# Batch 0 through the general attention path, four heads of batch 1's keys pooled on GpSimd in the head, and first value products in single PSUM banks

## The chip, the core and the metric

The kernel runs on one core of a Trainium2 chip. The core has a matrix engine (TensorE, PE in the profile, with its weight loads as PEld), a vector engine (DVE), a scalar engine (ACT), GpSimd (POOL) and a queue engine (SP). PE writes only to PSUM, which the kernel uses as four tiles of one bank (p1a to p1d) and two tiles of two banks each (p2, named p in the profile). Loads that change fp32 to bf16 on the way are issued by GpSimd; SP issues loads and stores without a change of type. The metric is the device time of one execution in microseconds, the median over several runs; lower is better.

## The reference

Eight batches, eight heads, 576 rows, head size 64. Keys and values are averaged over groups of 8 rows, so that 72 remain; attention is taken against these, and a mixer over tokens and channels follows. Cut to what matters:

```python
k_p = k.reshape(B, H, 72, 8, D).mean(axis=3)
v_p = v.reshape(B, H, 72, 8, D).mean(axis=3)
attn = softmax(q @ k_p.transpose(0, 1, 3, 2) / sqrt(D))
x = (attn @ v_p).transpose(0, 2, 1, 3).reshape(B, S, H * D)
h = relu(x.transpose(0, 2, 1) @ w_tok1) @ w_tok2        # tokens: 576 -> 256 -> 576
u = x + h.transpose(0, 2, 1)
out = u + relu(u @ w_ch1) @ w_ch2                       # channels: 512 -> 1536 -> 512
```

## The kernel before

All engines run an order written out by hand: the program emits steps one after the other, and each engine carries out its own instructions in just that order, waiting by semaphores for the others. The order comes from two tables. `HEAD` (line 21) lists what comes first: loads (words with L), dummy matmuls that keep PE busy (d with a count), and the whole attention and token mixing of batch 0. `PLAN` (line 22) has one row per unit. Unit n is the channel mixing of batch n (a ninth unit takes the last 64 rows of all batches together). It issues 12 tiles of the first layer, `l1_tile` (line 514, matmuls on line 517), and then 84 groups of quarter products of the second layer (line 583), which use sums and differences of halves so that fewer products are needed. Each of its `yield`s has a number, and the row of `PLAN` says which steps of the next batches are emitted at that number: "1.s0" is step s0 of batch 1. Unit n carries the attention of batch n + 1 and the pooling of batch n + 2.

Steps of a batch, by their names in both tables:

- `lk`, `lq`, `lv`: GpSimd issues the loads of keys, queries and values (lines 118 and 128). At a key or value load a second, small transfer brings rows 64 to 72.
- `K0`, `K1`, `V0`, `V1`: pooling of four heads by three adds on GpSimd (`pool8`, lines 171 to 180); `v1` is the same on DVE. `kpool` (line 250) pools all keys by 8 matmuls with the identity on PE, `vpool` (line 259) four heads of values.
- `Q0`, `Q1`: one block transpose on DVE for four heads of queries (line 284). `kpT`: four PE transposes of the pooled keys, copied by ACT (line 219).
- `s0`, `s1`, `s2`: scores and exponentials (line 289). Each takes both p2 tiles; its matmuls use four groups of 32 rows of the PE array (line 297). s0 and s1 do columns 0 to 384 of heads 0 to 3 and 4 to 7, s2 the last 192 columns of all heads.
- `av`: products with the values, with the division by the row sums on DVE (lines 370 to 387). In the head these go by four heads: `a00` is group 0, row chunks 0 and 1 (`avh`, line 325), `m01` the matching part of the token layer (`ath`, line 348). `X` and `A` (lines 464 to 480) make the transposed input of unit 0, with PE adding x and the token layer in PSUM.
- `w0` to `w3`: differences of halves of w_ch2 on DVE (line 563); "=1" to "=4": sums of halves of the hidden layer (line 552). `g`: a gate, by which GpSimd waits for a point in DVE's order (line 715).

Batch 0 has its own path to the scores. SP loads two pairs of heads of the queries as fp32 (line 742), ACT and DVE turn them to bf16 (c0 and c1, line 694), and GpSimd loads the other two pairs (line 700). PE pools the keys (`kp2`, line 227) and transposes them against a zero-padded tile (`kt2`, line 238), so that even and odd rows of a pair have their own stationary tile. PE transposes the queries too (`qT`, line 271), and `score` (line 309) does one pair of heads and one parity with two matmuls and one exponential.

Queues: GpSimd issues nearly all loads, in the order of the L words and of the `l` steps, mixed with its pooling and gates. SP has only the two fp32 loads in the head, and later the stores. The L words of the head are, in order: keys in three pieces (kA, kT, kB), late queries, values in three pieces, w_tok1 (four transfers), batch 1's keys, w_tok2, and then parts of w_ch1 and w_ch2 among batch 1's queries and values.

Of the kernel before, what the change touches and what calls it, by code (L numbers as in the profile page):

```python
# [8 lines left out]
FP32 = mybir.dt.float32  # L9
BF16 = mybir.dt.bfloat16  # L10
U32 = mybir.dt.uint32
AF = mybir.ActivationFunctionType
ALU = mybir.AluOpType
# [7 lines left out]
HEAD = """LkA LkT LkB Lq LvA LvT LvB Lt1 Lk1 Lt2 Lc1a Lq1 Lc1b Lc1c Lv1 Lc2b Lc1d p1 Lc2a Lc2c d4 c0 prep d3 c1 d4 d2 d1 q0 d2 kp0 kp1 kt0 q1 kt1 o0 kp2 o1 q3 e1 kt2 e0 q2 e3 vpool0 o3 d1 d1 a00 e2 vpool1 o2 a02 m01 d1 a04 m00 a12 m03 X1 m02 a10 m04 X0 p0 a14 1.kpool m11 m12 m14 m13 m10 A1 X3 A0 X2 A2 A3"""  # L21
PLAN = [
# [13 lines left out]
def kernel(  # L36
# [60 lines left out]
    qf = area2[:, 0:4 * BR * D].bitcast(FP32).rearrange("p (a n) -> p a n", a=2)  # L97
    f2 = area2[:, 2304:2304 + 2 * S].rearrange("p (c n) -> p c n", c=2)
    warm = area2[:, 3584:4096]
# [3 lines left out]
    kpz = area[0:SP, 0:1536].rearrange("j (h e d) -> j h e d", h=H, e=3)  # L103
    kT = area[:, 2048:2048 + 2 * H * SP].rearrange("m (o k) -> m o k", o=2)
    qT0 = area[:, 3200:3200 + 2 * HP * EV].rearrange("m (a l n) -> m a l n", a=HP, l=2)

# [23 lines left out]
    def first_kv(key, part):  # L130
        if (0, key) not in loaded:
            loaded[0, key] = raw.tile([SP, H, POOL, D], BF16, name=key + "r")
        h0, h1, j0, j1 = {"A": (0, HP, 0, BP), "B": (HP, H, 0, BP), "T": (0, H, BP, SP)}[part]
        kv(loaded[0, key], k if key == "k" else v, 0, h0, h1, j0, j1)

    def q_pairs(a0, a1):
        return q[0, 2 * a0:2 * a1].rearrange("(a l) (p r) d -> (l p) a (r d)", l=2, r=BR)
# [49 lines left out]
    def batch_steps(b):  # L187
# [5 lines left out]
        def prepare():  # L193
            kp = att.tile([SP, 2, 2, 4, D // 2], BF16, name="kp") if b >= 1 else None
            st.update(kp=kp, vp=values[par], ex=exps[par], xt=rests[b // 2 % 2])
            if not first:
                st["kD"] = att.tile([P, 2, 2, SP], BF16, name="kD")
# [20 lines left out]

        def kpT():
            ps = take([P, 4, SP], BF16)  # L220
            for i in range(4):
                nc.tensor.transpose(out=ps[:, i, :], in_=st["kp"][:, i // 2, i % 2].rearrange("j l d -> j (l d)"),
                                    identity=ident[0:SP, 0:SP])
            nc.scalar.copy(out=st["kD"].rearrange("p g e j -> p (g e j)"), in_=ps.rearrange("p i j -> p (i j)"))
            give(ps)

        def kp2(h0, h1):
            def go():
                ps = take([P, 512], FP32)
                n = (h1 - h0) * D  # L230
                for i in range(POOL):
                    nc.tensor.matmul(out=ps[0:SP, 0:n], lhsT=ident[0:SP, 0:SP], rhs=loaded[b, "k"][:, h0:h1, i, :],
                                     start=(i == 0), stop=(i == POOL - 1))
                nc.vector.tensor_copy(out=kpz[:, h0:h1, 1, :], in_=ps[0:SP, 0:n].rearrange("j (h d) -> j h d", d=D))
                give(ps)
            return go

        def kt2(h0, h1):
            def go():
                ps = take([P, 2, h1 - h0, SP], BF16)  # L240
                for odd in range(2):
                    for h in range(h0, h1):
                        nc.tensor.transpose(out=ps[:, odd, h - h0, :],
                                            in_=kpz[:, h, 1 - odd:3 - odd].rearrange("j e d -> j (e d)"),
                                            identity=ident[0:SP, 0:SP])
                nc.vector.tensor_copy(out=kT[:, :, h0 * SP:h1 * SP], in_=ps.rearrange("m o h j -> m o (h j)"))
                give(ps)
            return go
# [10 lines left out]
        def ppool(g):  # L259
            def go():  # L260
# [7 lines left out]
                give(ps)  # L268
            return go

        def qT(hp):
            def go():
                ps = take([P, NE, 2, BP], BF16)
                for rr in range(NE):
                    nc.tensor.transpose(out=ps[:, rr].rearrange("m l p -> m (l p)"),
                                        in_=loaded[b, "q"][:, hp, rr * P:(rr + 1) * P], identity=ident)
                nc.vector.tensor_copy(out=qT0[:, hp].rearrange("m l (r p) -> m r l p", p=BP), in_=ps)
                give(ps)
            return go
# [29 lines left out]
        def score(hp, odd):  # L309
            n = OD if odd else EV  # L310

            def go():
                ps = ps_two.tile([P, 2, 512], FP32, name="p2")
                exv = st["ex"][:, 0:H * S].rearrange("j (h n) -> j h n", h=H)[:, 2 * hp:2 * hp + 2]
                for hl in range(2):
                    h = 2 * hp + hl
                    keys = slice(h * SP, (h + 1) * SP)
                    nc.tensor.matmul(out=ps[0:SP, hl, 0:n], lhsT=kT[:, odd, keys], rhs=qT0[:, hp, hl, 0:n],
                                     start=True, stop=True)
                dst = exv.rearrange("j h (r p) -> j h r p", p=BP)[:, :, odd:BR:2, :]  # L320
# [466 lines left out]
```

## Time and profile before

| what | value |
|---|---|
| median of 3 runs | 265.07 us (264.4 to 265.51) |
| the profiled execution | 264.03 us |
| its span, first to last instruction | 262.2 us |
| granted TensorE clock | 1.00 |
| DMA, mean over the span | 131 GB/s, 34.29 MB |
| DMA from 20 to 50 us | 205 to 207 GB/s |
| chain that ended last | PE 80%, GpSimd 8%, DMA 7%, DVE 3% |

How to read the views: a line of the chain of waits has the start, the length and the work that the end of the kernel hung on at that time. A line of the timeline has the start, the busy time, engine, source line, operation, output and input tiles, their shapes and a count; in brackets stands how long the engine had been idle and what ended that. Busy time is not time on the path: matmuls overlap, so that one of 512 columns is shown as 379 ns while the next starts 216 ns after it. Rows of 40 digits cut the span into slices of 6.55 us, and each digit is the busy share in tenths. The time of a load "to landing" is counted from its issue.

### The profile page before, as it was taken

To read this page: it belongs to the slowest core of one execution; us is meant where nothing else is said; L and a number is where in the kernel's file an instruction comes from. 1 tells how busy PE (TensorE), PEld (TensorE's weight loads), DVE (VectorE), ACT (ScalarE), POOL (GpSimd) and SP (SyncE) were. 2 spreads that over 40 slices of the span, in tenths; PEclk is the share of its full clock that TensorE was granted. 3 is DMA by queue.
4 is the path that set the end of the run, shared out by engine and by line. 5 is a ranking of instruction groups with operands and counts; after the bars stand their busy time and mean duration, and the time that the engine had idled before them with its cause. 6 is when DMAs were issued, how large, how long until landed. Compare 5 with 4: busy or idle time off the path is not lost.

```text
span 262.2 us, 5324 instructions
## 1 busy us (share of the span) xinstructions
PE 255.8 (98%) x2121; PEld 160.4 (61%) x2121; DVE 179.7 (69%) x370; ACT 119.2 (45%) x195; POOL 150.0 (57%) x177
## 2 busy tenths in 40 slices
PE   8899999999999999999999999999999999999994
PEld 3775556754658545864487448744774486486483
DVE  4566489998786657993899449964795486175183
ACT  2445754149465554435641584155535502612610
POOL 8576145999989999999939881988000000101000
PEclk9999999999999999999999999999999999999999
DMA  7999999992096839699357840831414054503204
GB/s 150 191 200 205 206 206 208 207 223 77 2 172 101 133 118 201 146 196 261 66 154 125 239 133 2 162 92 41 123 35 127 5 158 113 129 0 88 75 0 160
DMA packets 31704, 34.29 MB, mean 131 GB/s; under 512 B 3136, under 2 KB 23744, under 8 KB 31680
## 3 DMA queue, kind: packets, MB, share of 16 engines
q0 software_dynamic: 17632, 17.64, 42.6%
q1 hardware_dynamic: 13632, 15.93, 20.4%
q10 hardware_dynamic: 416, 0.39, 0.5%
q8 instruction: 16, 0.26, 0.4%
q14 instruction: 8, 0.07, 0.1%
HBM read 38.99 MB, written 12.58 MB: 197 GB/s over the span
## 4 chain that ended last, share of the span: by engine, by line
PE 80%; POOL 8%; DMA 7%; DVE 3%; issue 1%; POOLq 0%
PE p1d L517 9%; PE p1c L517 9%; PE p1a L517 8%; PE p1b L517 7%; PE p1b L583 7%; PE p1c L583 7%; PE p1a L583 6%; DMA qb<-in_q_dram 5%; PE p1d L583 4%; PE p L297 3%; PE p L379 3%; POOL t L174 2%; POOL t L175 2%; DMA kr<-in_k_dram 2%; PE p L583 2%; PE p1d L393 2%
## 5 line engine op out<-in xcount | busy, mean ns | idle before, releaser
L717 POOL COPY flag<-flag 1x1 f32<-1x1 f32 x47 | 12.6, 269 | 94.5 <-DVE flag L716 94.5
L517 PEld LDWEIGHTS <-w_ch 128*128 128x128 bf16 x432 | 39.6, 98 | 43.4 <-issue 1.8
L583 PEld LDWEIGHTS <-area 128*128 128x128 bf16 x432 | 40.9, 98 | 7.4 <-issue 1.2
L306 ACT ACTIVATE ex<-p 72x768 bf16<-72x768 f32 x42 | 31.6, 803 | 15.9 <-PE p L297 15.7
L583 PEld LDWEIGHTS <-GT 128*128 128x128 bf16 x324 | 30.8, 98 | 8.2 <-issue 2.4
L175 POOL TENSOR_TENSOR t<-t 72x512 f32<-72x512 f32 x23 | 31.0, 1346 | 1.8
L521 ACT ACTIVATE GT<-p1d 128x512 bf16<-128x512 f32 x29 | 17.3, 597 | 27.0 <-PE p1d L517 21.4
L517 PE MATMUL p1d<-uT,w_ch 128*128 128x512 bf16 x104 | 28.8, 379 | 0.0
L174 POOL TENSOR_TENSOR t<-kr 72x1024 f32<-72x1024 bf16 x12 | 25.9, 2155 | 0.5
L517 PE MATMUL p1c<-uT,w_ch 128*128 128x512 bf16 x96 | 26.1, 379 | 0.0
L521 ACT ACTIVATE GT<-p1b 128x512 bf16<-128x512 f32 x26 | 15.6, 598 | 23.2 <-PE p1b L517 16.8
L517 PE MATMUL p1a<-uT,w_ch 128*128 128x512 bf16 x92 | 25.3, 379 | 0.0
L517 PE MATMUL p1b<-uT,w_ch 128*128 128x512 bf16 x92 | 24.2, 379 | 0.0
L174 POOL TENSOR_TENSOR t<-vr 72x1024 f32<-72x1024 bf16 x11 | 24.1, 2187 | 0.3
L521 ACT ACTIVATE GT<-p1a 128x512 bf16<-128x512 f32 x26 | 15.5, 596 | 11.8 <-PE p1a L517 9.2
L521 ACT ACTIVATE GT<-p1c 128x512 bf16<-128x512 f32 x27 | 16.1, 598 | 8.7 <-PE p1c L517 8.3
L384 DVE TENSOR_TENSOR x<-p,den 128x512 bf16<-128x512 f32 x28 | 19.4, 692 | 1.0
L557 DVE TENSOR_TENSOR area<-GT 128x1536 bf16<-128x1536 bf16 x9 | 9.8, 1086 | 12.4 <-ACT GT L521 12.4
L545 DVE TENSOR_TENSOR area<-GT 128x1536 bf16<-128x1536 bf16 x9 | 10.6, 1178 | 10.1 <-ACT GT L521 7.7
L379 PEld LDWEIGHTS <-ex 72*128 72x128 bf16 x280 | 13.4, 98 | 5.6 <-DVE flag L716 0.4
L583 PE MATMUL p1c<-area,area 128*128 128x256 bf16 x120 | 15.4, 273 | 0.0
L379 PE MATMUL p<-vp,ex 72*128 72x65 bf16 x280 | 14.6, 194 | 0.0
(188 smaller groups left out, 461.1 us busy)
## 6 DMA issues: line engine op xcount, KB each, us to landing
out_dram<-o SPq DMA_DIRECT2D x32, 256.0 KB, 4.0
qb<-in_q_dram POOLq DMA_DIRECT2D x7, 576.0 KB, 9.3
kr<-in_k_dram POOLq DMA_DIRECT2D x7, 512.0 KB, 7.4
vr<-in_v_dram POOLq DMA_DIRECT2D x7, 512.0 KB, 9.8
w_ch<-in_moe_w_ch_dram POOLq DMA_DIRECT2D x5, 512.0 KB, 15.8
mem<-u SPq DMA_DIRECT2D x10, 256.0 KB, 2.0
v<-mem SPq DMA_DIRECT2D x20, 128.0 KB, 2.8
area<-in_q_dram SPq DMA_DIRECT2D x2, 288.0 KB, 3.0
```

The costliest lines, as they stand in the source:

```text
L174: eng.tensor_tensor(out=t4[:, 0:n], in0=t[:, hs, 0:4], in1=t[:, hs, 4:8], op=ALU.add)
L175: eng.tensor_tensor(out=t4[:, 0:n, 0:2], in0=t4[:, 0:n, 0:2], in1=t4[:, 0:n, 2:4], op=ALU.add)
L297: nc.tensor.matmul(out=pss[l // 2][0:SP, l % 2, o:o + n1 - n0], lhsT=st["kD"][quad, g, db, :], rhs=st["qD"][quad, g, n0:n1, db], start=(db ...
L306: nc.scalar.activation(out=dst, in_=src, func=AF.Exp, scale=scale)
L379: nc.tensor.matmul(out=ps[:, h // 4, (h % 4) * (D + 1):(h % 4 + 1) * (D + 1)], lhsT=st["ex"][:, h * S + n0:h * S + n0 + P], rhs=st["vp"][: ...
L384: nc.vector.tensor_tensor(out=dst.rearrange("p (a h d) -> p a h d", a=2, d=D), in0=view[:, :, :, 0:D], in1=den[rows, :, :, None].broadcast ...
L517: nc.tensor.matmul(out=ps, lhsT=w_ch1[:, kk, m * P:(m + 1) * P], rhs=uT[kk], start=(kk == 0), stop=(kk == 3))
L521: nc.scalar.activation(out=GT[:, m, :], in_=ps, func=AF.Relu)
L545: nc.vector.tensor_tensor(out=out, in0=a, in1=b, op=ALU.subtract)
L557: nc.vector.tensor_tensor(out=S4[:, 0], in0=GT[:, f, hi], in1=GT[:, sec, hi], op=ALU.add)
L583: nc.tensor.matmul(out=ps[i] if split else ps[:, i], lhsT=chunk(u, i, a(m)), rhs=w(m), start=start and m == 0 and (i == 0 or split), stop= ...
L717: nc.gpsimd.tensor_copy(out=flag[:, 1:2], in_=flag[:, 0:1])
```

## The change

Batch 0 loses its own path and goes by `Q`, `kpT` (in two halves, h0 and h1) and `s0` to `s2` like the others. SP now loads the fp32 keys of heads 0 to 3 (tile `kf`, in two transfers: rows 0 to 64 and 64 to 72), and DVE pools them from there by three adds (k0). GpSimd loads all queries of batch 0 in two pieces (Lqa, Lqb) and the keys of heads 4 to 7, which PE pools (kp2). Batch 1's keys are pooled half by PE in the head (1.kp2 in place of 1.kpool) and half by GpSimd in the head (1.K0, after p1 and before the issues of the last four weight loads). The first value product (f00 in place of a00) writes each row chunk to its own one-bank tile, with its own reciprocal and product on DVE. The head's order and all rows of `PLAN` are new; the steps in `PLAN` are the same as before, with three gates fewer. Loads in the head: w_tok2 now comes before batch 1's keys, c1b before batch 1's queries, and c1d before c2b. The diff, cut to its core:

```diff
-HEAD = """LkA LkT LkB Lq LvA LvT LvB Lt1 Lk1 Lt2 Lc1a Lq1 Lc1b Lc1c Lv1 Lc2b Lc1d p1 Lc2a Lc2c d4 c0 prep d3 c1 d4 d2 d1 q0 d2 kp0 kp1 kt0 q1 kt1 o0 kp2 o1 q3 e1 kt2 e0 q2 e3 vpool0 o3 d1 d1 a00 e2 vpool1 o2 a02 m01 d1 a04 m00 a12 m03 X1 m02 a10 m04 X0 p0 a14 1.kpool m11 m12 m14 m13 m10 A1 X3 A0 X2 A2 A3"""
+HEAD = """Lqa LkB LkT Lqb LvT LvA prep LvB Lt1 Lt2 Lk1 Lc1a Lc1b Lq1 Lc1c Lv1 p1 1.K0 Lc1d Lc2b Lc2a Lc2c d4 k0 d4 d2 d2 d3 h0 Q0 s0 kp2 Q1 h1 d2 s2 vpool0 d2 a02 f00 vpool1 s1 m03 a04 m01 X0 m02 a10 p0 m04 m00 X1 a12 a14 m11 m10 A0 1.kp2 m12 m13 m14 X2 A1 A2 X3 A3"""
 PLAN = [
-    {0: "0.u3 1.Q0 2.lk 1.kpT", 3: "0.u1", 4: "1.s0 g g", 5: "1.Q1", 9: "1.s1 0.u0", 10: "1.vpool1 1.vpool0 g", 11: "1.s2", 12: "=3 0.u2 2.lq", 13: "1.av1", 14: "1.av3", 16: "1.av2", 18: "w0 3.lk", 19: "1.av0 3.lq", 20: "1.av4 w1 g", 23: "1.at1 2.lv", 24: "1.at0 3.lv =1", 25: "=2 =4", 26: "g", 28: "w3", 31: "1.u1 1.u2", 32: "1.t1", 33: "1.t2 w2", 34: "2.K0", 35: "1.u0", 38: "3.Q1 2.K1", 40: "1.u3", 41: "1.t0", 42: "g", 43: "2.Q0 1.t3", 44: "1.u4 2.V0 2.kpT"},
+    {0: "0.u0 2.lk g 0.u3", 1: "1.kpT", 2: "1.Q0", 3: "g", 4: "2.lq", 6: "2.lv 1.s0", 9: "1.Q1 0.u2", 10: "1.s1", 11: "0.u1 1.vpool1 1.s2", 12: "1.vpool0 =3", 13: "1.av1", 15: "1.av3 3.lv", 16: "1.av2 w0", 20: "g 3.lq 1.av0", 21: "1.av4", 22: "w1 g", 23: "=1 1.at0", 24: "=2 3.lk 1.at1", 25: "w3", 26: "g =4", 28: "2.K0 2.K1", 31: "1.u3", 33: "1.u0", 34: "1.u1", 35: "2.V0", 36: "w2", 37: "1.t3", 40: "1.u2", 42: "1.t0 2.Q0", 43: "1.t2 1.t1", 44: "1.u4"},
...
+    kf = area2[0:SP, 0:2 * HP * POOL * D].bitcast(FP32).rearrange("j (h i d) -> j h i d", i=POOL, d=D)
...
+    def q_group(b, g):
+        return q[b, 4 * g:4 * g + 4].rearrange("l (j n) d -> (l j) (n d)", n=2 * BR)
...
+        def kpT_half(g):
+            def go():
+                ps = take([P, 2, SP], BF16)
+                for e in range(2):
+                    nc.tensor.transpose(out=ps[:, e, :], in_=st["kp"][:, g, e].rearrange("j l d -> j (l d)"),
+                                        identity=ident[0:SP, 0:SP])
+                nc.scalar.copy(out=st["kD"][:, g], in_=ps)
+                give(ps)
+            return go
...
+        def kp_sbuf():
+            pool8(nc.vector, kf, slice(0, HP), st["kp"][:, 0], True)
+
+        def kp_psum():
+            ps = take([P, 512], FP32)
+            for i in range(POOL):
+                nc.tensor.matmul(out=ps[0:SP, 0:HP * D], lhsT=ident[0:SP, 0:SP], rhs=loaded[b, "k"][:, HP:H, i, :],
+                                 start=(i == 0), stop=(i == POOL - 1))
+            nc.vector.tensor_copy(out=st["kp"][:, 1].rearrange("j e l d -> j e (l d)"),
+                                  in_=ps[0:SP, 0:HP * D].rearrange("j (n e) -> j e n", e=2))
+            give(ps)
...
+        def avh_one(g, c):
+            def go():
+                for cc in (c, c + 1) if c < 4 else (4,):
+                    ps = take([P, 4, D + 1], FP32)
+                    den = outp.tile([P, 2, 4], FP32, name="den", bufs=4)
+                    for h in range(4):
+                        n0 = (4 * g + h) * S + cc * P
+                        nc.tensor.matmul(out=ps[:, h, :], lhsT=st["ex"][:, n0:n0 + P], rhs=st["vp"][:, 4 * g + h, :],
+                                         start=True, stop=True)
...
+                    nc.vector.reciprocal(out=den[rows, 0], in_=ps[rows, :, D])
+                    nc.vector.tensor_tensor(out=dst[:, g * 256:(g + 1) * 256].rearrange("p (h d) -> p h d", d=D),
+                                            in0=ps[rows, :, 0:D],
+                                            in1=den[rows, 0, :, None].broadcast_to([rows.stop, 4, D]), op=ALU.mult)
+                    give(ps)
+            return go
...
+        name["k0"], name["kp2"] = kp_sbuf, kp_psum
...
+    def first_q(g):
+        nc.gpsimd.dma_start(out=quarters(loaded[0, "q"])[:, g], in_=q_group(0, g))
...
-        for a in range(2):
-            nc.sync.dma_start(out=qf[:, a:a + 1, :], in_=q_pairs(a, a + 1))
+        for j0, j1 in ((0, BP), (BP, SP)):
+            nc.sync.dma_start(out=kf[j0:j1].rearrange("j h i d -> j h (i d)"),
+                              in_=k[0, 0:HP].rearrange("h (j i) d -> j h (i d)", i=POOL)[j0:j1])
```

Removed with it: `kp2`, `kt2`, `qT`, `score` and the tiles `kpz`, `kT` and `qT0` of batch 0's own path, the two casts c0 and c1, and two of DVE's memsets. The rows of units 1 to 8 of `PLAN`, cut here, hold the same steps in another order. Of these, the prediction speaks of 2.kpT, which moves from step 44 of unit 0 to step 0 of unit 1.

More of the change, by code (lines that the diff above doesn't have):

```diff
@@ L96 @@
     area2 = early.tile([P, 6 * 1024], BF16, name="area2")
-    qf = area2[:, 0:4 * BR * D].bitcast(FP32).rearrange("p (a n) -> p a n", a=2)
-    f2 = area2[:, 2304:2304 + 2 * S].rearrange("p (c n) -> p c n", c=2)
-    warm = area2[:, 3584:4096]
+    kf = area2[0:SP, 0:2 * HP * POOL * D].bitcast(FP32).rearrange("j (h i d) -> j h i d", i=POOL, d=D)
+    f2 = area2[:, 4608:4608 + 2 * S].rearrange("p (c n) -> p c n", c=2)
+    warm = area2[:, 4096:4608]
     uT_tails = singles.tile([P, 4, 4 * P], BF16)
@@ L102 @@
     area = early.tile([P, 6 * 1024], BF16, name="area")
-    kpz = area[0:SP, 0:1536].rearrange("j (h e d) -> j h e d", h=H, e=3)
-    kT = area[:, 2048:2048 + 2 * H * SP].rearrange("m (o k) -> m o k", o=2)
-    qT0 = area[:, 3200:3200 + 2 * HP * EV].rearrange("m (a l n) -> m a l n", a=HP, l=2)
     values = [singles.tile([SP, H, D + 1], BF16, name=f"vp{i}") for i in range(2)]
@@ L132, in first_kv @@
             loaded[0, key] = raw.tile([SP, H, POOL, D], BF16, name=key + "r")
-        h0, h1, j0, j1 = {"A": (0, HP, 0, BP), "B": (HP, H, 0, BP), "T": (0, H, BP, SP)}[part]
+        h0, h1, j0, j1 = {"A": (0, HP, 0, BP), "B": (HP, H, 0, BP), "T": (HP * (key == "k"), H, BP, SP)}[part]
         kv(loaded[0, key], k if key == "k" else v, 0, h0, h1, j0, j1)
-    def q_pairs(a0, a1):
-        return q[0, 2 * a0:2 * a1].rearrange("(a l) (p r) d -> (l p) a (r d)", l=2, r=BR)
+    def q_group(b, g):
+        return q[b, 4 * g:4 * g + 4].rearrange("l (j n) d -> (l j) (n d)", n=2 * BR)
     def load(key, b):
@@ L193, in prepare @@
         def prepare():
[L194 to L197, printed above, removed]
+            st.update(kp=att.tile([SP, 2, 2, 4, D // 2], BF16, name="kp"), vp=values[par], ex=exps[par],
+                      xt=rests[b // 2 % 2], kD=att.tile([P, 2, 2, SP], BF16, name="kD"))
         def late(key):
@@ L225, in kpT @@
             give(ps)
[L227 to L248, printed above, removed]
+        def kp_sbuf():
[8 more added lines that the diff above has]
+            give(ps)
         def kpool():
@@ L267, in go @@
                 (nc.scalar.copy if first and g else nc.vector.tensor_copy)(out=st["vp"][:, hs, 0:D], in_=view)
[L268 to L277, printed above, removed]
                 give(ps)
@@ L307, in scores @@
             return go
[L309 to L320, printed above, removed]
-                src = ps[0:SP, :, 0:n].rearrange("j h (r p) -> j h r p", p=BP)
-                nc.scalar.activation(out=dst, in_=src, func=AF.Exp, scale=scale)
-            return go
         def avh(g, c):
@@ L345, in go @@
                                             op=ALU.mult)
+            return go
[8 more added lines that the diff above has]
+                                         start=True, stop=True)
+                    rows = slice(0, P) if cc < 4 else slice(0, BP)
+                    dst = late("x")[:, cc] if cc < 4 else st["xt"][rows]
+                    nc.vector.reciprocal(out=den[rows, 0], in_=ps[rows, :, D])
[3 more added lines that the diff above has]
+                    give(ps)
             return go
@@ L487, in batch_steps @@
                 name[t + str(g)] = pool(nc.vector, t, g)
-        for hp in range(HP):
-            if hp < 3:
-                hs = ((0, 2), (2, 4), (4, 8))[hp]
-                name[f"kp{hp}"], name[f"kt{hp}"] = kp2(*hs), kt2(*hs)
-            name[f"q{hp}"], name[f"o{hp}"], name[f"e{hp}"] = qT(hp), score(hp, 1), score(hp, 0)
+        for g in range(2):
+            name[f"h{g}"] = kpT_half(g)
+        name["k0"], name["kp2"] = kp_sbuf, kp_psum
         for i in range(3):
@@ L497, in batch_steps @@
             for g in range(2):
-                name[f"a{g}{c}"], name[f"m{g}{c}"] = avh(g, c), ath(g, c)
+                name[f"a{g}{c}"], name[f"f{g}{c}"], name[f"m{g}{c}"] = avh(g, c), avh_one(g, c), ath(g, c)
         for c in range(6):
@@ L691, in head @@
             batches[1][0]()
-        elif s[0] == "c":
-            a = int(s[1:])
-            (nc.vector.tensor_copy if a % 2 else nc.scalar.copy)(out=loaded[0, "q"][:, a, 0:BR * D], in_=qf[:, a, :])
         else:
@@ L697, in head @@
             batches[int(b)][1][s]()
-    def late_q():
-        nc.gpsimd.dma_start(out=loaded[0, "q"][:, 2:HP, 0:BR * D], in_=q_pairs(2, HP))
-    early_loads = {"q": late_q, "t1": load_tok1, "t2": load_tok2, }
+    def first_q(g):
+        nc.gpsimd.dma_start(out=quarters(loaded[0, "q"])[:, g], in_=q_group(0, g))
+    early_loads = {"qa": lambda: first_q(0), "qb": lambda: first_q(1), "t1": load_tok1, "t2": load_tok2, }
     for key in "kv":
@@ L740 @@
         nc.vector.memset(warm, 0.0)
-        for a in range(2):
-            nc.sync.dma_start(out=qf[:, a:a + 1, :], in_=q_pairs(a, a + 1))
+        for j0, j1 in ((0, BP), (BP, SP)):
+            nc.sync.dma_start(out=kf[j0:j1].rearrange("j h i d -> j h (i d)"),
+                              in_=k[0, 0:HP].rearrange("h (j i) d -> j h (i d)", i=POOL)[j0:j1])
         qb = loaded[0, "q"] = raw.tile([P, HP, BR * D + D], BF16, name="qb")
-        nc.vector.memset(qb[:, :, BR * D:], 0.0)
-        nc.vector.memset(kpz, 0.0)
         nc.vector.memset(w_tok1[:, 4:6, :], 0.0)
```

16 rows, old and new, of the table PLAN are left out of this document.

## The prediction

> **What bounds the kernel now.** Read first: the page's totals. Second: the chain of waits, cut to the first 30 us. Third: the timeline from 24 to 57 us, with the landing time of every load.
>
> ```profile
> span 262.2 us, 5324 instructions
> PE 255.8 (98%) x2121; PEld 160.4 (61%) x2121; DVE 179.7 (69%) x370; ACT 119.2 (45%) x195; POOL 150.0 (57%) x177
> DMA  7999999992096839699357840831414054503204
> ```
>
> PE (TensorE) is never idle, and the DMA engines are full for the first nine slices (9 x 6.55 = 59 us). The list of waits shows one PE wait after 24 us, of 0.4 us. So the end is the moment at which unit 0 starts, plus a stream of about 234 us that both kernels issue (the two PLANs hold the same steps; only three gates fewer), plus whatever PE is made to wait in it.
>
> ```profile
> 2.03 5.57 DMA kr<-in_k_dram
> 7.74 0.61 PE p1d L232 x8
> ...
> 19.34 1.73 PE p1b L253 x8
> ...
> 23.91 0.43 PE p1b L476 x2
> 24.35 0.43 PE p1c L517 x2
> ```
>
> Unit 0 starts at 24.35. From 7.74 the chain is nearly all PE: the head is PE bound once the first keys have landed.
>
> ```profile
> 38.68 0.95 DVE L545 TENSOR_TENSOR area<-w_ch 128x1536 bf16<-128x1536 bf16 x1
> ...
> 41.48 0.96 DVE L545 TENSOR_TENSOR area<-w_ch,area 128x1536 bf16<-128x1536 bf16 x1
> ...
> 45.97 0.06 DVE L716 MEMSET flag<- 1x1 f32 x1
> 46.11 0.83 POOL L717 COPY flag<-flag 1x1 f32<-1x1 f32 x1 [0.29 <-DVE flag L716]
> ```
>
> This is unit 0's second bound. Issue start plus time to landing gives, per load: first keys 7.6, q1 23.7, third w_ch1 part 27.7, v1 31.0, c1d 35.9, c2a 38.4, c2c 41.0 (24.0 + 17.0). Their users start at 31.50 (values of batch 1), 36.94 (l1 tile 8), 38.68 (w0) and 41.48 (w1): slacks of 0.5, 1.0, 0.3 and 0.5 us. DVE then runs without a break to the gate at 45.97. GpSimd pools 2.K0 and 2.K1 behind it until 56.39, where 2.kpT waits about 0.3 us for it. A head that is shorter by G gets all of G only if these places let it through.
>
> **The change, part by part.**
>
> *PE work in the head.* Out (pieces of the chain): key sums 0.61 + 0.45 + 0.88 = 1.94; key transposes 0.24 + 0.17 + 0.26 = 0.67; query transposes 4 x 0.28 = 1.12; scores L318 2.48; 1.kpool 1.73; sum 7.94. In: s0, s1, s2 at 0.47 each (L297) 1.41; kp2 0.88; 1.kp2, half of 1.kpool, 0.87; four transposes of 72 columns 0.13; sum 3.29. PE work falls by 4.65 us. Both heads spend 19 dummies.
>
> *Loads.* Equal bytes: 576 KB of fp32 go through SP either way (queries before, keys now), and queries and keys swap 288 KB on GpSimd's queue. Nine slices at the same fullness: v1, c2a and c2c end the same sums as before, so I leave them at 31.0, 38.4 and 41.0. q1 goes behind c1b (about 25), k1 behind t2 (19.7, where t2 ended), c1d ahead of c2b (33.3). Could they come earlier? q1 took 23.7 - 21.0 = 2.7 us for 576 KB, k1 with its tail 18.6 - 14.9 = 3.7; 288 KB more by the first rate and less by the second would be 0.5 us. Bounds: 0.5 earlier, 0.2 later; taken: 0.
>
> *Vector pooling of four heads (k0).* Not in the trace from fp32. The nearest adds with two SBUF inputs ran beside GpSimd's adds:
>
> ```profile
> 58.79 2.22 DVE L174 TENSOR_TENSOR t<-vr 72x1024 f32<-72x1024 bf16 x1
> 61.05 1.10 DVE L175 TENSOR_TENSOR t<-t 72x512 f32<-72x512 f32 x1
> 62.19 2.23 DVE L180 TENSOR_TENSOR vp<-t 72x256 bf16<-72x256 f32 x1
> ```
>
> Upper bound 5.55. Lower: L626's 0.410 for 256 and 0.685 for 512 fp32 elements are 1.07 ns each plus 0.135, so 1.23 + 0.68 + 0.41 = 2.3. In the head GpSimd issues loads and adds nothing, and that cost a two-input DVE add nothing here:
>
> ```profile
> 34.48 0.74 POOL L128 DMA_DIRECT2D qb<-in_q_dram  x1 [0.34 <-ACT GT L521]
> 34.51 0.96 DVE L545 TENSOR_TENSOR area<-GT 128x1536 bf16<-128x1536 bf16 x1 [0.64 <-ACT GT L521]
> ```
>
> (beside a GpSimd add at 49.41, L545 took 1.78). Taken: 2.35.
>
> *The key tile on SP, by a page.* The Trainium skill (DMA: Bandwidth & Descriptors, § Why a DMA increments its semaphore by 16 and not by 1) says that a DMA issued from SP uses the largest number of engines up to 16 that divides its slowest dimension, so the eight last key rows would go over 8 engines; no run here shows it. At that page's 27 GiB/s per engine I estimate 0.3 us for their 64 KB against 0.15; the forecast would not move, since k0 has more room than that (next part).
>
> *The head as it should now run.* Keys land as the queries did, 4.4; k0 4.5 to 6.85; qa, first on GpSimd's queue, about 7.1 (256 KB landed there at 6.94); Q0 (0.76, L284) to 7.9; s0 8.0 to 8.5; two exps (1.50, L306) to 10.1. Second half: keys 8.7, PE sum 9.6, DVE cast 10.1, qb 10.5 (the old late queries closed the same sum), Q1 11.3, s2 11.35, exps 11.9 to 13.4. vA and vT 12.3, sum and cast 13.6; a02 on PE 13.65, its DVE pair (0.21 + 0.69) to 15.05; f00 in two single banks, 2 x (0.16 + 0.41) = 1.14 against 0.90, to 16.2. s1 needs both two-bank buffers, so it waits for a02's product: 15.1, exps to 17.15. That wait is the new bound: PE idles, and a10, a12, a14 with their products follow to 20.1 (DVE). 1.kp2 waits for k1, 19.75 to 20.6; m12 to m14 21.3; relu on ScalarE and DVE 22.25; A2, X3, A3 23.4. Unit 0 starts at 23.4: G = 0.95, of 4.65 us of PE work saved. k0 is free up to 3.95 us: then s0's exps still end at 11.35, when Q1 lets s2 go.
>
> *GpSimd in the head.* 1.K0: 2.12 + 1.27 + 0.84 and gaps, 4.4 us, from 19.7 to 24.1, and 1.kpT reaches PE at 23.4 + 1.7 = 25.1: free, 1.0 us of cover; beyond that, each us costs one. Queued behind 1.K0 are the issues of c1d, c2b, c2a, c2c and batch 2. In flight at 19.7: c1a, c1b, q1, c1c and v1, 2.2 MB, 11 us of a full DMA; c1d is issued at 24.1. Nothing starves.
>
> *Unit 0.* The value sums come after two more steps (start + 8.1 instead of + 7.15): 31.5 against v1's 31.0, free. w0 still follows av2 on DVE, which arrives at 37.8 and waits for c2a to 38.45: 0.23 ahead of the old 38.68 and no more. Queued behind w0: the products of av0 and av4, which end 0.23 early, at 41.21. at0's fifth matmul (42.04 before, 41.09 now) waits 0.15. w1, the sums and the gate stay 0.23 early, so 2.K1 ends at 56.16. PE reaches 2.kpT, moved behind two matmuls of 0.43 in all, at 55.7 and waits. Before, kpT and those two matmuls were done at 56.39 + 0.13 + 0.43 = 56.95; now at 56.16 + 0.13 = 56.29. **G is cut to 0.66.** Later units: PE dense before, same work, 0.
>
> Sum: span 262.2 - 0.7 = 261.5; with the 1.8 us around the span (264.03 - 262.2) 263.4 for the profiled execution. That one stood 1.0 under the median of the runs, so I forecast **264.4**. With k0 at 5.55 it is 1.4 us more, with loads 0.5 early 0.3 less.
>
> **The rivals.**
>
> *Loads early.* If the loads come 1 us sooner than the sums of bytes say and the head loses its wait at s1 (unit 0 at 22.4), about 1.9 us pass: 263.2; with 2.5, 262.6. For: queries arrive faster than keys. Against: the fullness of the DMA row; w0's slack was 0.3.
>
> *DVE bound (slower than before).* k0 runs at the rows beside GpSimd, 5.55. It decides from 3.95: s2 waits for s0's exps, everything after it is 1.4 to 1.6 late, unit 0 starts at 24.8, 0.45 later than now: 265.5. Against: the row at 34.51.
>
> *GpSimd late (slower).* In its queue 2.K0 now has 3.lk as its last load ahead, and each issue waits for the load eight before it (the second half of 2.lk, 27.92, for the third w_ch1 part, landed 27.7). 3.lk's halves wait so for 2.lk, 43.9, free before the gate at 45.7. If the wait is for 2.lv (49.5) instead, 2.K0 starts at 50.2, not 46.7, and 2.kpT 3.5 late, 2.8 net of G: 267.2. A half pool out of place in a later unit costs the same kind of price, 4.4 less its slack. Against: the waits at 10.79, 12.22, 18.72 and 24.00 all fit eight.
>
> *Half clock (slower).* Matmuls of 512 columns start 0.43 us apart until about 5.2 us and 0.216 after. PE now waits often from 6.4 to 13.6. If the clock falls there, 3.3 us of work take twice as long: about +2.5, 267. Against: PE stood still for about 1 us before 7.7 and stayed fast. By the Trainium skill (TensorE: Matmul & The Clock Gate, § Part 1) an idle window of about 3.4 us is needed, and the longest wait above is 1.1; by that rule this rival is out.
>
> **How the numbers follow.** A measurement here can tell about 0.5%, 1.3 us. Forecast 0.50, loads early 0.23, DVE bound 0.10, GpSimd late 0.13, half clock 0.04. Faster by over 0.5%: 0.21 of loads early and 0.05 of the forecast, 0.26. Slower: 0.12 + 0.04 + 0.03 = 0.19. Same: 0.55. The range, 262.5 to 266.2, takes in most of loads early, DVE bound and the start of GpSimd late.
>
> **What would show it.** k0's first add near 1.2 us; first exp at 8.6 instead of 9.9; s1's matmuls waiting on DVE's x at 15; L517 first at 23.4; w0 on DVE idle until a w_ch landing near 38.4; 2.K1 ending near 56.2; PE dense after 57. Wrong if unit 0 starts before 22.9 with c2a landed by 37.5, or if PE shows waits of over 1 us after 60.

## The result, and the profile after

The changed kernel takes **274.12 us** (272.71 to 275.81, 6 runs) against 264.80 (263.47 to 265.51, 6 runs): a ratio of 1.0358, 95% interval 1.0301 to 1.0415. It is slower by 3.6%, 7.9 us above the upper end of the range. The profiled execution has a span of 273.1 us, 10.9 more than before.

The page of the changed kernel, totals and slices:

```profile
span 273.1 us, 5248 instructions
...
PE 259.0 (95%) x2089; PEld 160.6 (59%) x2089; DVE 174.9 (64%) x362; ACT 118.9 (44%) x194; POOL 150.8 (55%) x177
...
PE   7399999999999999979999999999999999999994
...
PEclk9855999999999999999999999999999999999999
```

PE does 32 matmuls fewer and yet is busy 3.2 us longer. The third and fourth slice say why: the clock granted to it is half, from about 11 to 28 us. Slice 2 of the PE row (3) is an idle stretch ahead of that, and slice 18 (7) a second one, at 118 us. The chain of waits gives the first one's cause:

```profile
0.74 0.76 SPq L722
1.55 6.83 DMA area<-in_k_dram
8.48 1.23 DVE t L170
9.73 0.70 DVE t L171
...
11.62 0.86 PE p L280 x8
```

The second of SP's two key transfers, 64 KB for the rows 64 to 72, was issued at 1.55 and landed at 8.38. The first, 512 KB, took 5.2 us by the view of its line and landed at 5.95. DVE's pooling of four heads (k0) starts only with both. PE's timeline and the windows of the head (busy time of PE, PEld, DVE, ACT and POOL, then the granted clock, the DMA share and GB/s):

```profile
5.32 0.81 PE L666 MATMUL p1a<-area 128*128 128x512 bf16 x3
10.93 0.24 PE L217 MATMUL p1b<-ident,kp 72*128 72x72 bf16 x2 [4.80 <-DVE kp L174]
```

```profile
5.00:10.00 5.00, 1.13 (x6) 0.29 (x3) 1.49 (x2) 0.00 (x0) 2.31 (x4) 1.00 1.36 174
10.00:15.00 5.00, 3.10 (x21) 1.84 (x22) 2.16 (x5) 1.78 (x3) 3.09 (x5) 0.62 1.48 172
15.00:20.00 5.00, 5.00 (x43) 3.02 (x42) 0.92 (x3) 1.78 (x3) 4.93 (x7) 0.50 1.26 202
25.00:30.00 5.00, 5.00 (x49) 4.17 (x47) 3.03 (x8) 1.16 (x2) 4.84 (x8) 0.68 1.22 204
```

The dummies are done at 6.1, PE waits 4.80 us, and then matmuls take about twice as long: by the pieces of the chain s0 takes 0.86 instead of the 0.47 of the same shapes before, a value sum 1.85 instead of 0.87. The first matmuls of unit 0, before and after, in PE's timelines:

```profile
24.18 0.59 PE L517 MATMUL p1c<-uT,w_ch 128*128 128x512 bf16 x2
...
32.30 0.59 PE L500 MATMUL p1b<-uT,w_ch 128*128 128x512 bf16 x2
```

Unit 0 starts at 32.30 against 24.18 (24.35 by the chain): 8.1 of the 10.9 us. The other 2.8 come after it; the list of PE's waits (total, times, longest) names where:

```profile
PE p1b L217 <- DVE kp L174: 4.8, 1, 4.8
PE p1a L566 <- DVE flag L696: 1.9, 1, 1.9
...
PE p1d L400 <- DVE u L401: 0.7, 1, 0.7
```

The wait of 1.9 is in unit 2. It ends with DVE, which stood still itself. The timelines of DVE, of SP and of GpSimd there:

```profile
114.74 0.06 DVE L696 MEMSET flag<- 1x1 f32 x1
119.35 0.45 DVE L443 STREAM_TRANSPOSE uT<-v 128x256 uint32<-128x256 uint32 x1 [3.94 <-DMA v<-mem]
```

```profile
109.41 0.83 SPq L419 DMA_DIRECT2D mem<-u  x2
112.68 1.80 SPq L431 DMA_DIRECT2D v<-mem  x4
```

```profile
113.79 0.75 POOL L124 DMA_DIRECT2D qb<-in_q_dram  x1
```

Some blocks of u are transposed by way of DRAM: SP writes them out (L419), waits until they have landed, reads them back in another order (L431), and DVE's block transposes (L443, step T) finish them. I call this the bounce. The read-back of batch 3 was issued 1.1 us ahead of a query load of 576 KB (5.lq) and value loads of 576 KB behind it, and landed so late that DVE waited 3.94 us. DVE works in order, so the sums of unit 2's second layer stood behind T2, and PE behind them.

So there are two stories. **Head**: late keys, an idle PE, half clock. **Unit 2**: a read-back that shares the DMA engines with large loads. The rival to both is that something else in the new head (the pooling on DVE, many short matmuls, the small waits between them) or in the new PLAN costs the time.

### The profile page after: what moved, and what is told of

Its sections match the earlier page's. It is cut to its first block, busy times and chain, and to the rows that moved or that the text cites. A ratio compares the mean times of both kernels' runs of the same rounds, so it can differ in the third digit from the quotient of the medians.

```text
span 273.1 us, 5248 instructions
## 1 busy us (share of the span) xinstructions
PE 259.0 (95%) x2089; PEld 160.6 (59%) x2089; DVE 174.9 (64%) x362; ACT 118.9 (44%) x194; POOL 150.8 (55%) x177
## 4 chain that ended last, share of the span: by engine, by line
PE 75%; DMA 11%; DVE 6%; POOL 4%; SPq 1%; issue 1%; ACT 1%; DVEq 0%; POOLq 0%; ACTq 0%
PE p1a L500 8%; PE p1d L500 8%; PE p1b L500 7%; PE p1c L500 7%; PE p1b L566 6%; PE p1c L566 5%; PE p1d L566 5%; DMA v<-mem 4%; PE p L280 4%; PE p1a L566 3%; PE p L364 3%; DMA mem<-u_tails 3%; DMA area<-in_k_dram 3%; PE p1c L378 2%; PE p L566 2%; POOL t L170 2%
## 5 line engine op out<-in xcount | busy, mean ns | idle before, releaser
L289 ACT ACTIVATE ex<-p 72x768 bf16<-72x768 f32 x48 | 36.1, 802 | 18.3 <-PE p L280 18.2
L500 PE MATMUL p1a<-uT,w_ch 128*128 128x512 bf16 x108 | 29.2, 379 | 0.0
L170 POOL TENSOR_TENSOR t<-kr 72x1024 f32<-72x1024 bf16 x13 | 28.2, 2167 | 1.5 <-DMA kr<-in_k_dram 1.0
L504 ACT ACTIVATE GT<-p1a 128x512 bf16<-128x512 f32 x30 | 17.9, 597 | 20.2 <-PE p1a L500 19.8
L500 PE MATMUL p1d<-uT,w_ch 128*128 128x512 bf16 x96 | 26.0, 379 | 0.0
L500 PE MATMUL p1b<-uT,w_ch 128*128 128x512 bf16 x96 | 25.6, 379 | 0.0
L504 ACT ACTIVATE GT<-p1c 128x512 bf16<-128x512 f32 x24 | 14.3, 597 | 21.0 <-PE p1c L500 21.0
L500 PE MATMUL p1c<-uT,w_ch 128*128 128x512 bf16 x84 | 22.9, 380 | 0.0
L504 ACT ACTIVATE GT<-p1d 128x512 bf16<-128x512 f32 x27 | 16.1, 597 | 10.9 <-PE p1d L500 8.2
L540 DVE TENSOR_TENSOR area<-GT 128x1536 bf16<-128x1536 bf16 x9 | 9.0, 996 | 11.7 <-ACT GT L504 11.7
L528 DVE TENSOR_TENSOR area<-GT 128x1536 bf16<-128x1536 bf16 x9 | 8.7, 965 | 9.5 <-ACT GT L504 9.5
L280 PE MATMUL p<-qD,kD 32*72 32x384 bf16 (+1 forms) x256 | 13.8, 313 | 0.4 <-DVE qD L267 0.4
```

The costliest lines, as they stand in the source:

```text
L170: eng.tensor_tensor(out=t4[:, 0:n], in0=t[:, hs, 0:4], in1=t[:, hs, 4:8], op=ALU.add)
L280: nc.tensor.matmul(out=pss[l // 2][0:SP, l % 2, o:o + n1 - n0], lhsT=st["kD"][quad, g, db, :], rhs=st["qD"][quad, g, n0:n1, db], start=(db ...
L289: nc.scalar.activation(out=dst, in_=src, func=AF.Exp, scale=scale)
L500: nc.tensor.matmul(out=ps, lhsT=w_ch1[:, kk, m * P:(m + 1) * P], rhs=uT[kk], start=(kk == 0), stop=(kk == 3))
L504: nc.scalar.activation(out=GT[:, m, :], in_=ps, func=AF.Relu)
L528: nc.vector.tensor_tensor(out=out, in0=a, in1=b, op=ALU.subtract)
```

## The experiments

In the table, "keys" is the start of k0's first add, "half clock" the first stretch at half clock by half-microsecond windows, "rest" the span less the start of unit 0, and the last column PE's longest wait after that start; these four are from the profiled execution of each kernel. Ratios are against the kernel before, run on the same chip beside it. Runs 4 and 5 had two executions each, the profiled one first, that differ by the mean granted clock (0.954 and 1.000 in run 4, 0.962 and 0.973 in run 5), so no ratio is given.

| kernel | us | ratio (95%) | keys | half clock | unit 0 | rest | wait |
|---|---|---|---|---|---|---|---|
| before | 264.8 | 1 | none | none | 24.18 | 238.0 | 0.4 |
| changed | 274.12 | 1.0358 (1.0301 to 1.0415) | 8.48 | 11.2 to 28.2 | 32.30 | 240.8 | 1.9 |
| 1 old head, new PLAN | 263.48 | 0.9959 (0.9930 to 0.9987) | none | none | 24.70 | 237.2 | 0.2 |
| 2 new head, old PLAN | 273.72 | 1.0340 (1.0279 to 1.0402) | 8.53 | 10.9 to 27.9 | 32.18 | 239.8 | 1.4 |
| 3 fill | 273.87 | 1.0348 (1.0194 to 1.0502) | 8.40 | 114.9 to 121.7 | 26.33 | 244.2 | 4.6 |
| 4 two halves | 275.37, 265.75 | | 5.83 | 9.3 to 26.3 | 30.22 | 243.4 | 3.3 |
| 5 GpSimd's keys first | 274.55, 270.10 | | 6.93 | 9.8 to 26.8 | 30.82 | 242.0 | 2.4 |
| 6 small piece first | 273.32 | 1.0314 (1.0210 to 1.0418) | 7.57 | 11.2 to 28.3 | 31.69 | 241.6 | 2.6 |
| 7 before, cold | 270.32 | 1.0212 (1.0151 to 1.0272) | none | (text) | 26.28 | 242.1 | 3.1 |
| 8 halves and fill | 274.44 | 1.0367 (1.0311 to 1.0423) | 6.27 | 113.5 to 123.7 | 24.99 | 247.7 | 8.5 |
| 9 bounce | 272.45 | 1.0281 (1.0225 to 1.0338) | 8.31 | 8.9 to 29.4 | 32.76 | 238.1 | 0.5 |
| 10 fill and bounce | 267.25 | 1.0116 (1.0067 to 1.0166) | 7.95 | none | 25.52 | 238.3 | 0.4 |
| 11 halves, fill, bounce | 266.75 | 1.0106 (1.0014 to 1.0197) | 6.59 | none | 25.30 | 239.8 | 1.1 |

**Head or PLAN** (1 and 2). Each kernel takes one table from before and one from the change, with the code that it needs.

> The kernel before with its own head and the rows of PLAN of the changed kernel. Plan theory (2.8 us of the loss lie in the new order of units 1 to 8, the wait at 118 us among them): time near 267.5, TensorE waits of 2 to 3 us in all after 60 us. Rival (the late waits come from the late head only): 264.3 to 265.3, no such waits.

> The changed kernel's head with the PLAN of before, the other corner beside the old head with the new PLAN (0.996 of before). Theory A (the late keys and the half clock of the new head cost 8 us, whatever follows): unit 0 starts at 32 to 33, 272 us or more. Rival D (the new head only loses with the new PLAN's later units): unit 0 at 32 but the rest catches up, 268 us or less.

The new PLAN with the old head is the best kernel of all, by 0.4% (0.1 to 0.7), a little below both theories; the new head with the old PLAN loses the whole 3.4%. The PLAN is not at fault, and theory A holds for the head. That the rest costs 2.8 us only with the new head is open after these two.

**Fill** (3). Dummies keep PE busy until the pooled keys are there:

```diff
-... d4 k0 d4 d2 d2 d3 h0 Q0 ...
+... d4 k0 d4 d2 d2 d3 d4 d4 d4 d4 d4 d2 h0 Q0 ...
```

> The changed kernel with 22 more dummy matmuls ahead of the first key transposes, so that TensorE stays busy while it waits for the key tile. Clock theory (the head lost about 5 us because TensorE ran at half clock from 11 to 27 us after standing still for 4.8 us): granted clock full throughout, the keys still late at 8.4 us, unit 0 starts near 27.4 us instead of 32.5, time near 269. Rival (the head is long through waits on DVE and the loads, and the clock is only a sign of it): unit 0 within 1 us of 32.5, time 273 to 274.

The head did what the theory said: keys as late as ever, clock full, unit 0 at 26.33. So the half clock costs 32.30 - 26.33 = 6.0 us. The total did not move, because the bounce in unit 2 now stopped PE for 4.6 us and the clock fell there, for 6.8 us. Whoever goes by the total alone throws the right theory away.

**Why the keys are late** (4, 5, 6). The key tile in two transfers of 72 rows and 2 heads; GpSimd's key loads ahead of its first query load; the small transfer ahead of the large:

```diff
-for j0, j1 in ((0, BP), (BP, SP)):        # rows 0:64 and 64:72, 4 heads each
+for h0 in (0, 2):                         # 4: heads 0:2 and 2:4, 72 rows each
...
-Lqa LkB LkT Lqb
+LkB LkT Lqa Lqb                           # 5
...
-for j0, j1 in ((0, BP), (BP, SP)):
+for j0, j1 in ((BP, SP), (0, BP)):        # 6
```

> The changed kernel with the fp32 key tile loaded by SP in two transfers of 72 rows and two heads each, in place of rows 0 to 64 and rows 64 to 72. Small-piece theory (the transfer of 8 rows is what lands at 8.4 us): the tile is there by 5.5 to 6 us, TensorE waits about 2 us instead of 4.8 and keeps its clock, unit 0 starts at 24.5 to 26, time 265.5 to 268. Sharing theory (SP's packets take turns with the larger query packets of GpSimd's queue, whatever the pieces): the tile at 7.5 us or later, the clock falls, time within 1.5 us of 274.

> The changed kernel with GpSimd's first loads in the order keys, key rest, queries, queries, so that SP's key tile competes with key packets as the old fp32 queries did. Sharing theory: the SP tile lands by 6 us; the first queries land near 8.9, so s0 starts near 9.8 and TensorE stands still about 3.5 us; time 266 to 270 if the clock holds. Small-piece theory: the tile still lands after 8 us, time 273 to 275.

> The changed kernel with SP's transfer of the 8 last key rows issued ahead of the one of 64 rows. Theory S (a transfer of 8 rows is slow by its shape, beside GpSimd's loads): it lands at 6 us or later again, the 64 rows at 6 to 7 us, and the first pooling add starts with the later of the two, at 6.5 to 8.5. Theory Q (it was slow because it stood behind 512 KB in SP's own queue): it lands by 4 us, the 64 rows at about 6, the first add at 6.0 to 6.3, as with two transfers of 72 rows. Either way TensorE is idle for 1.5 us or more and the clock may fall: 265 to 274 us.

With two equal halves (run 4) the same 576 KB are there at 5.8, 2.6 us sooner, as the small-piece theory said; its hope for the clock failed in the profiled execution. Run 5 fits neither of its theories: 6.9 is after 6 and before 8. In run 6, with the small piece first, the keys are there at 7.5, and now it is the large piece that ends the wait (issued at 1.20, 6.27 us). Neither theory of run 6 fits alone: the second of the two transfers is the late one in either order, and the split into 64 and 8 rows is worse than the split into halves in both.

The packet records of the traces narrow it. Before, 547 of SP's 576 KB were under way when GpSimd's first packet started (3.60), and SP's last packet ended at 4.02. In the changed kernel 490 KB were under way at GpSimd's first packet (4.43). The rest went beside GpSimd's packets until 6.25, the last eight of the 4-byte packets that close SP's transfers (16 and 8 of them) took 0.58 to 0.87 us each in place of 0.01, up to 7.05, and the landing came at 8.38. In run 6 SP and GpSimd ran side by side for longer: from 4 to 5 us, 60 packets of 2 KB and 58 of 2.25 KB started. Another order of GpSimd's loads alone brought the keys 1.55 us sooner (run 5), so GpSimd's queue is part of the cause. But the halves of run 4 were through at 5.07 with only 374 KB under way at GpSimd's first packet (3.67). Why they pass so much better, and why the closing packets and the landing of the 8 rows are slow, is not settled.

Run 4 shows more of the clock. PE waited for only 1.41 and 0.85 us, and in the profiled execution the clock fell all the same; the other execution took 265.75 us at full clock. The window of 3.41 us ahead of the fall, with PE busy for 1.27 of it:

```profile
5.85:9.26 3.41, 1.27 (x7) 0.51 (x6) 3.02 (x4) 0.28 (x1) 1.32 (x3) 1.00 1.14 187
```

**The clock in the unchanged kernel** (7). The 14 dummies ahead of the first query transposes are left out; nothing else.

```diff
-... Lc2c d4 c0 prep d3 c1 d4 d2 d1 q0 ...
+... Lc2c c0 prep c1 q0 ...
```

> The kernel before without the 14 dummy matmuls ahead of its first query transposes, all else as it was: TensorE idles until 5.9 us. Theory A (an idle TensorE takes the clock to half for a time, and that is most of the changed kernel's loss): the granted clock is 0.5 when the key sums start at 7.7, each takes about 0.9 to 1.2 instead of 0.61 us, unit 0 starts 3 to 8 us later than 24.35, time 268 to 273. Rival E (the clock follows something else in the new head, such as the DVE pooling or the many short matmuls): clock full from about 8 us, unit 0 within 1 us of 24.4, time 264 to 266.

PE's timeline of this kernel:

```profile
4.47 0.71 PE L275 MATMUL p1a<-ident,qb 128*128 128x128 bf16 x5 [4.47 <-ACT qb L694]
...
7.20 1.06 PE L232 MATMUL p1c<-kr,ident 72*72 72x128 bf16 x8 [1.16 <-DMA kr<-in_k_dram]
8.05 1.06 PE L232 MATMUL p1d<-kr,ident 72*72 72x128 bf16 x8
...
10.35 1.92 PE L232 MATMUL p1d<-kr,ident 72*72 72x256 bf16 x8
```

The key sums take 1.06 instead of 0.61 us, and matmuls run at half rate until about 13; unit 0 starts 2.1 us late, less than theory A's lower end of 3. The profile's clock column reads 1.00 all the while: it shows the clock being taken away, not a start from idle, so the durations have to be read too. That the time, 270.32, lies inside theory A's range is luck, since the rest lost 4.1 us more by the other mechanism: a bounce in the old PLAN, whose write took 4.88 us (132.19 to 137.07) instead of 3.06, so that its read-back was issued 0.02 us behind a query load instead of 2.6 ahead. PE waited 3.15 us and the clock fell from 146.4 to 149.8.

**Halves and fill** (8), with 18 more dummies where PE waited in run 4 (the expectations of runs 8 and 11 say 17; the last group is of 4, not 3):

```diff
-... d2 d2 d3 h0 Q0 s0 kp2 Q1 h1 d2 s2 ...
+... d2 d2 d3 d4 d3 h0 Q0 d4 s0 kp2 Q1 d3 h1 d2 d4 s2 ...
```

> The changed kernel with two edits in the head: the fp32 key tile in two transfers of 72 rows by 2 heads, and 17 more dummy matmuls in the places where TensorE waited in the run with these transfers (7 ahead of h0, 4 between Q0 and s0, 3 ahead of h1, 3 more behind it). Theory A (the loss in the head is the late keys, 2.6 us, plus the half clock that the wait brings, 6 us, and nothing else): keys at about 5.8, the granted clock stays full from 5 us on, unit 0 starts between 24 and 25, the head costs nothing against the kernel before; if unit 2's bounce stalls as in the run with fill alone, 2 to 5 us more, otherwise 264 to 266 us. Rival B (the many small waits of this head throttle the clock whatever the fill): a granted clock of 0.5 to 0.7 between 10 and 25 us, unit 0 at 29 or later, 270 us or more.

In the head theory A holds: clock full, unit 0 at 24.99, within 0.8 of before. Then the bounce took nearly all of it back: unit 0 starts 7.3 us sooner than in the changed kernel and the rest is 6.9 longer, far above the 2 to 5 us that theory A allowed for a stall. Waits of PE, SP's queue, and GpSimd's load:

```profile
PE p1b L566 <- DVE flag L696: 8.5, 1, 8.5
```

```profile
102.12 0.85 SPq L419 DMA_DIRECT2D mem<-u  x2
107.03 2.00 SPq L431 DMA_DIRECT2D v<-mem  x4
```

```profile
106.55 0.76 POOL L124 DMA_DIRECT2D qb<-in_q_dram  x1
```

**The bounce** (9, 10). The loads of batches 5 and 6 go behind T2, alone and with the fill:

```diff
-26: "=2 5.lq 3.M0 =4", ... 29: "3.T2 5.lv", ... 33: "6.lv 6.lq", ... 38: "3.T1", 40: "4.av1"
+26: "=2 3.M0 =4", ... 29: "3.T2", ... 38: "3.T1 5.lq 5.lv", 40: "4.av1 6.lv 6.lq"
```

> The changed kernel with the loads of batches 5 and 6 moved as before and nothing else: the fourth corner beside fill alone (273.9) and both (267.2). Theory A: head as in the changed kernel (unit 0 at 32.3, half clock to 27 us), no long wait in unit 2, so 237.5 to 239 us from there, span 270 to 271.5, time 271.5 to 273.3. Rival: the bounce stalls at the half clock's later start all the same, 274 or more.

> The changed kernel with the 22 extra dummies of the first experiment and, in the third row of the PLAN, the four loads of batches 5 and 6 behind T2's read-back of the bounce (5.lq from step 26 and 5.lv from step 29 to step 38, 6.lv and 6.lq from 33 to 40). Theory A (the stall in unit 2 comes from GpSimd's 576 KB and 512 KB loads that share the DMA engines with the bounce): the read-back lands in 2 to 3.5 us instead of 6 to 9, TensorE's wait of 4.6 us before the last layer of unit 2 falls below 1.5, the span from unit 0 on is 237 to 239 instead of 244 us, and the time falls from 274 to 266 to 269 us. Rival C (the bounce is slow by itself, as its write already took 3.1 instead of 2.1 us with nothing of GpSimd's in flight): the stall stays at 3 us or more and the time at 272 to 275.

Both came out as theory A had it, but for the half clock of run 9, which lasted to 29.4 instead of 27. DVE's timeline in run 10, and its page:

```profile
110.65 0.45 DVE L443 STREAM_TRANSPOSE uT<-v 128x256 uint32<-128x256 uint32 x1 [2.02 <-DMA v<-mem]
```

```profile
span 263.8 us, 5267 instructions
...
PEclk9999999999999999999999999999999999999999
```

The two edits together are worth 274.12 - 267.25 = 6.9 us; alone they are worth 0.3 (fill) and 1.7 (bounce), and the intervals of the ratios overlap with that of the changed kernel in both cases. The profiled executions say why the sum is more than its parts: fill alone starts unit 0 6.0 us sooner, but the rest grows from 240.8 to 244.2 us by the longer stall and the half clock that follows it; the moved loads alone take the rest to 238.1, but leave the head as it was.

How the race in unit 2 is run shows across the kernels with the new PLAN. In all of them but the last three the query load is issued 4.4 us after the write; the lead is what the write leaves of that:

| kernel | write to read-back, us | lead over the load | DVE's wait |
|---|---|---|---|
| 1 | 2.75 | 1.66 | 1.10 |
| 4 | 2.85 | 1.57 | 5.35 |
| 5 | 2.99 | 1.42 | 1.45 |
| 6 | 3.02 | 1.39 | 4.62 |
| changed | 3.27 | 1.11 | 3.94 |
| 3 | 3.83 | 0.59 | 6.61 |
| 8 | 4.91 | -0.48 | 10.47 |
| 9, 10, 11 (loads behind) | 3.01, 3.59, 4.67 | over 5 | 1.41, 2.02, 3.12 |

With the loads out of the way a slow write costs only its own length; with them the wait goes from 1.1 to 10.5, though a lead of 1.4 to 1.6 can go either way. Why the write takes 2.75 in one kernel and 4.91 in another stays open; in run 8 the DMA engines moved 15 GB/s on average in the last 2 us of it (105 to 107), so it was not for want of bandwidth. The wait of 2.4 us in run 5 is another of the kind: it is in unit 3, and DVE had waited 5.18 us for the read-back of the last 64 rows, issued at 119.45, 1.4 us behind another query load (118.01).

**All three mendings** (11): run 8's head with the moved loads.

> All three mendings on the changed kernel: the key tile in two transfers of 72 rows, 17 more dummies where TensorE waited, and the four loads of batches 5 and 6 behind unit 2's bounce. Theory A (late keys, half clock and this bounce are all of the loss): unit 0 at about 25.0 as with the first two mendings, no wait over 2 us after it, 237 to 239 us from there, so a span of 262 to 264 and 264 to 266 us: level with before, not faster, since the new head with its queries at 9 us starts unit 0 no earlier than the old one's 24.35. Rival F (something more is lost): a wait over 2 us in another unit, 268 us or more.

```profile
span 265.1 us, 5260 instructions
...
PE   8999999999999999899989999999999999999994
...
PEclk9999999999999999999999999999999999999999
```

From unit 0 on no wait over 1.1 us is left and the clock is full, but the kernel is still 1.1% (0.1 to 2.0) slower than before, just above theory A's upper end (266.75 against 266; span 265.1 against 264). One of its four executions took 270.23 us with a mean clock of 0.987, so the clock is not safe even here. Of the 2.9 us of span that the profiled execution has more than before, 1.1 lie ahead of unit 0 and 1.8 behind it, where PE waits 1.1 us in unit 2 and 0.9 in unit 3.

## Why the prediction was wrong

**The step that failed** is "Keys land as the queries did, 4.4". The bytes through SP were equal, but not their split: two equal transfers before (landed at 3.64 and 4.35), 512 and 64 KB after, landed at 5.95 and 8.38. Nor was the company the same: 95% of the old queries were under way when GpSimd's first packet came, 85% of the new keys. Even in equal halves the keys took until 5.8 to 6.6. How the split and the company come to cost this much is known only in part (runs 4 to 6). The sentence on the Trainium skill's rule (eight engines for the 8 rows, 0.3 us instead of 0.15) looked at the right transfer and priced it at less than a twentieth of the 6.83 us that it took; the number of engines does not explain that.

**The rival that happened was named and thrown out with a number that hung on the failed step.** "The longest wait above is 1.1" was true of a head with keys at 4.4. With keys at 8.4 the wait is 4.8, and the half clock comes by the very rule quoted. The rule was also too kind: in run 4 the clock fell after waits of 1.41 and 0.85, and in run 9 with PE busy for 1.23 of the 3.41 us ahead of the fall. Its price was also too small: "3.3 us of work take twice as long", where 17 us ran at half clock, worth 6.0 us. The mechanism should have been priced over how long the clock stays down, not over the work near the wait.

**"PE dense before, same work, 0"** for the later units failed by 2.8 us. The moved step 5.lq was not costed: the old PLAN has it at step 44 of its row and the new one at 26, one step ahead of the read-back of the bounce. It cost nothing in run 1 (write 2.75, rest 237.2) and 1.9 to 8.5 us of PE's time in the changed kernel and in runs 3, 4, 6 and 8.

**Right were the smaller steps.** k0's three adds took 1.22, 0.69 and 0.42, 2.33 in all against 2.35 taken, so the slow bound of 5.55 and the rival "DVE bound" fall. GpSimd's pooling in the head ended at 24.05 in run 8, ahead of unit 0 at 24.99, so it was free as costed. The new PLAN lost nothing by itself (run 1). One reading was off by half a microsecond, without effect: before, the matmuls of 512 columns start 0.43 us apart only until 4.58, not 5.2.

**Unit 0 at 23.4** would not have come with a full clock either: 24.99 to 26.33 in the runs with fill. In run 11 the first scores stand at 10.14, not 8.0, since k0 started at 6.59 and Q0 follows it on DVE. The 4.65 us less of PE work bought nothing in any run: this head waits for transfers and for DVE.

By size, of the 10.9 us of span: 6.0 half clock in the head (run 3), 2.1 a head that is later even at full clock (26.33 - 24.18), 2.8 the bounce and smaller waits in later units (run 9 takes the rest back to 238.1).

## What to carry to other kernels

When PE work at the start is replaced by work of another engine, cost what keeps PE busy meanwhile: two waits of 2.3 us together cost 5.2 us through the clock (unit 0 at 30.22 in run 4, 24.99 in run 8), and dummies must last until the data is really there. On these traces the clock stayed wherever PE was busy for 1.5 us or more of each 3.41. When a load is moved in a hand-written order, look for a transfer that another engine waits for in order, and keep large loads off it. When two mendings each do little, run them together before giving either up.

## What the runs showed of the hardware

**The clock moves on a grid.** The edges come from half-microsecond windows of the changed kernel (granted clock third from the end): 0.66 means that the clock was full for 0.16 of 0.50 us, 0.77 that it came back 0.23 in.

```profile
11.00:11.50 0.50, 0.17 (x2) 0.04 (x2) 0.50 (x1) 0.28 (x1) 0.39 (x1) 0.66 1.60 158
28.00:28.50 0.50, 0.50 (x5) 0.34 (x3) 0.50 (x2) 0.00 (x0) 0.50 (x2) 0.77 1.22 201
```

From 11.16 to 28.23 are 17.07 us. Worked out in the same way, it is 17.07 in runs 2, 4, 5 and 6 too, 20.48 in run 9, 10.24 in run 8, 6.83 in run 3 and 3.42 in unit 3 of run 7: 5, 6, 3, 2 and 1 times 3.41. The Trainium skill (TensorE: Matmul & The Clock Gate, § Part 1) gives a free-running window of 3413 ns, and these lengths agree. It also says that an idle window takes the clock and a busy one gives it back. Here the measurement differs on both: a window need not be idle to lose the clock (see below), and in the head of the changed kernel it took five windows to come back, though the third of them was wholly busy. In unit 3 of run 7 one window gave it back:

```profile
17.99:21.40 3.41, 3.41 (x28) 2.54 (x26) 1.78 (x6) 0.34 (x1) 2.57 (x4) 0.50 1.53 176
...
146.40:149.81 3.41, 3.04 (x10) 1.42 (x10) 3.19 (x7) 0.60 (x1) 1.41 (x2) 0.50 0.82 147
```

What makes a window count as busy, when the head's many short matmuls do not and ten longer ones do, stays open.

**What PE does in a window decides, not the length of a wait.** The edges cut each of the 13 profiled executions into windows of 3.41 us. Of those at full clock, all 25 in which PE was busy for 1.42 us or less are followed by half clock (12 in the middle of a kernel, 13 at its end), and none with 1.46 or more is. Close to the border lie a window of run 4, which lost the clock, one of the changed kernel and one of the kernel before, which kept it:

```profile
115.07:118.48 3.41, 1.40 (x12) 1.10 (x13) 0.00 (x0) 1.50 (x2) 0.00 (x0) 1.00 1.06 207
...
116.97:120.38 3.41, 1.57 (x16) 1.19 (x13) 1.03 (x4) 1.50 (x2) 0.00 (x0) 1.00 1.04 212
...
257.25:260.66 3.41, 1.49 (x14) 1.07 (x11) 1.27 (x4) 0.00 (x0) 0.17 (x1) 1.00 0.87 301
```

So the wait of 1.9 us in unit 2 of the changed kernel cost no clock, and 1.41 with most of 0.85 in one window of run 4 did. The grid lies differently in each execution (the first fall in the head comes at 8.9 to 11.2 us), so the same waits can fall on either side; that this parts the two executions of run 4 is likely and not shown, since only one was profiled.

**SP's transfers are slow beside GpSimd's.** A read-back of 4 x 128 KB landed in 2.8 us in run 1 (lead 1.66; median of the four) and in 8.5 in run 8, issued 0.48 us behind a query load. By the Trainium skill (DMA: Bandwidth & Descriptors, § Queues, rings and completion order) each DMA engine takes turns between the queues by whole packets; that would slow both, and fits the direction. The 60 and 58 packets of run 6 agree with such turns; at the bounce no run here shows them.
